# Gated linear attention and a multiplicative feed-forward on one core: smaller weight units, an earlier x, and the output weight converted in part 1

## The chip, the cores and the metric

One NeuronCore of one Trainium2 chip runs the whole program in one launch. The metric is device time in microseconds (us); lower is better. Engines are called PE (TensorE, matmuls; PEld is its weight load), DVE (VectorE), ACT (ScalarE), POOL (GpSimd) and SP (SyncE, which here only issues transfers).

## The reference

Shapes: batch 4, 8 heads, 768 steps, head dimension 48; then 3072 tokens of width 384 and a hidden width of 1024. The weights come as float64, the rest as float32.

```python
for t in range(S):                                   # per batch and head
    state = alpha[t][:, None] * state + outer(k[t], v[t])
    y[t]  = q[t] @ state
x = y.transpose(0, 2, 1, 3).reshape(3072, 384)       # heads side by side
h = ((x @ w1) * (x @ w2)) @ w3
out = h @ w_out
```

## The kernel before

The work falls into three stages.

**Part 1, attention by chunks.** The steps are cut into 24 chunks of 128 (`N = 24`, six for each batch). A chunk `n` goes through helpers that the loop `for n in range(N)` calls for different chunks at once:

- `load_a` and `load` fetch alpha, k, q and v, 192 KB each, in rows of 192 bytes, several chunks ahead.
- `logs` (ACT, L227) takes the logarithm of alpha; `decays` (PE L235, ACT L238 and L239) sums it along the chunk with a triangular matrix and exponentiates it both ways; `decayed` (DVE L247) multiplies k and q with that into `qk`.
- `transposed` (PE L266, ACT L267) turns `qk` into `qkT`.
- `scores` (PE L305, DVE L308) multiplies k with q and masks the result into `ms`.
- `outer` and `advance` (PE L277, DVE L285 and L287, POOL) carry the state to the next chunk.
- `attend` (PE L324 and L327, ACT L331) gives the chunk's output `x`; PE L324 is the product with the state and is left out in the first chunk of a batch.
- `store_x` writes `x` to a DRAM buffer `xd`, one for every three chunks (a group `g` of 384 tokens), from SP's queue, one chunk late.

**Weights.** The float64 weights are read as pairs of 32-bit words and put together again as float32 by `to_fp32` (DVE L180, L183, L186, L187, L189; ACT L179, L184). A unit is 128 rows by `CW = 512` columns of one matrix. For w1 and w2, `load_gates` then splits the result into three parts (ACT L196, DVE L198 and L199), so that three float32r products give the precision of float32. A unit is a generator: `convert(steps)` advances up to three begun units by so many steps, a gate unit taking four after its load and the others three. The six units of the first 512 columns (three blocks of rows for each matrix) are needed before the first gate tile.

**Gates.** `load_x(g)` reads a group back from `xd` as `xT`, `split_x` cuts it into three parts (ACT L352, DVE L353 and L354), and `gate(g, f)` computes 128 of the 1024 hidden columns: two halves (one for each of w1 and w2), each with six matmuls (PE L363), an evacuation (ACT L365), three matmuls (PE L367) and a second evacuation (DVE L368), then the product (DVE L379) that `store_ab` writes to DRAM. In part 1 the list `fill` holds gate tiles, and `run(1)`, called twice in a chunk, does half a tile each time. `begin` says after which chunk a group is split: groups 0 to 4 at chunks 6, 10, 14, 18 and 22.

**Part 2.** The remaining gate tiles are done one after another. Beside them the units of the output weight (`load_out`, eight) and of w3 (`load_w3`, sixteen) are converted, at 2.7 steps a tile. As soon as 128 rows of w3 are there, `fold` transposes them (PE L406, ACT L408) and multiplies them with `wo` (PE L412, split by ACT L415 and DVE L416 and L417), so that w3 and w_out become one matrix `w3o`. When all eight folds are done, `load_ab` begins to read the products back.

**Last part.** For each of 24 token blocks: `split_ab` (ACT L430, DVE L431 and L432) and `project` (PE L363 and L367 with `w3o`, DVE L368), and the store of the output.

Each engine works through its instructions in order. The framework's scheduler decides how the helpers' instructions are interleaved on an engine, so the order is close to the program's but not equal to it. Transfers from SP go through one queue, in order.

Of the kernel before, what the change touches and what calls it, by code (L numbers as in the profile page):

```python
# [20 lines left out]
P = 4096.0  # L21
# [27 lines left out]
def kernel(  # L49
# [36 lines left out]
    xp = pool("xp", 1)  # L86
    tr = [pool("tr0", 1)]
    gw = pool("gw", 2)
    abp = pool("abp", 3)
    dram = pool("dram", 1, space=DRAM)  # L90
    ps = pool("ps", 8, space=PSUM)
    conversion = ExitStack()
    rawp = pool("rawp", 3, stack=conversion, side="right")
    cvt = pool("cvt", 3, stack=conversion, side="right")
    part1 = ExitStack()
    p1 = pool("p1", 1, stack=part1, side="right", reuse_waits="tile")
    inp = pool("inp", 3, stack=part1, side="right", reuse_waits="tile")
# [24 lines left out]
            st["a", n] = inp.tile([C, H, D], FP32, tag="ac", name="ac")  # L122
            nc.sync.dma_start(out=st["a", n], in_=rows(alpha, n))

    def load(n):
        if n >= N:
            return
        st["kq", n] = inp.tile([C, 2, H, D], FP32, tag="kq", name="kq")
        st["v", n] = vs[n % len(vs)]
        nc.sync.dma_start(out=st["kq", n][:, 0], in_=rows(k, n))  # L130
        nc.sync.dma_start(out=st["kq", n][:, 1], in_=rows(q, n))
        nc.sync.dma_start(out=st["v", n][:, :, 0:D], in_=rows(v, n))

    nc.scalar.preload_act_table_set(LN_EXP_SET)
    load_a(0)
    load(0)
    load_a(1)
    load(1)
    load_a(2)


    ident = const.tile([C, C], FP32, name="ident")
    rebias = const.tile([C, 1], FP32, name="rebias")

    w12 = [const.tile([C, 3, KM, DF], FP32R, name=f"w{i + 1}") for i in range(2)]

    utri = p1.tile([C, C], FP32, name="utri")
    after = p1.tile([C, C], FP32, name="after")
# [15 lines left out]
    for x in Ts + decs:  # L164
        nc.gpsimd.memset(x, 0.0)

    def to_fp32(dst, src):

        n = src.shape[1]
        raw = rawp.tile([C, n], I64, tag="raw", name="raw")  # L170
        nc.sync.dma_start(out=raw, in_=src)
        yield
        words = raw.bitcast(U32).rearrange("p (n w) -> p n w", w=2)
        low, high = words[:, :, 0], words[:, :, 1]

        mant = cvt.tile([C, n], FP32, tag="mant", name="mant")
        top = mant.bitcast(U32)
        rest = cvt.tile([C, n], FP32, tag="rest", name="rest", bufs=2)
        nc.scalar.activation(rest, low, AF.Copy, scale=2.0 ** -52)  # L179
        nc.vector.tensor_scalar(top, high, 0x000FFFFF, 0x00100000, op0=ALU.bitwise_and, op1=ALU.bitwise_or)  # L180

        power = cvt.tile([C, n], U32, tag="power", name="power", bufs=2)
        nc.vector.tensor_scalar(power, high, 20, 0x7FF, op0=ALU.logical_shift_right, op1=ALU.bitwise_and)  # L183
        nc.scalar.activation(power, power, AF.Relu, scale=2.0 ** 23, bias=rebias)  # L184
        yield
        nc.vector.scalar_tensor_tensor(mant, top, 2.0 ** -20, rest, op0=ALU.mult, op1=ALU.add)  # L186
        nc.vector.scalar_tensor_tensor(power, high, 0x80000000, power, op0=ALU.bitwise_and, op1=ALU.bitwise_or)  # L187
        to = mant if dst is None else dst()
        nc.vector.tensor_mul(to, mant, power.bitcast(FP32))  # L189
        yield  # L190
        return to

    def load_gates(i, src, kk, c0, n):
        w = yield from to_fp32(None, src[ds(kk * C, C), ds(c0, n)])
        h, l, m = (w12[i][:, x, kk, ds(c0, n)] for x in range(3))
        nc.scalar.activation(h, w, AF.Copy, scale=(1.0 - 2.0 ** -13) / P)  # L196
        yield
        nc.vector.scalar_tensor_tensor(l, h.bitcast(FP32), -P, w, op0=ALU.mult, op1=ALU.add)  # L198
        nc.vector.scalar_tensor_tensor(m, h.bitcast(FP32), P + 1.0, w, op0=ALU.mult, op1=ALU.subtract)  # L199

    weights, begun = deque(), deque()

    def convert(steps):

        for _ in range(steps):
            while weights and len(begun) < 3:
                begun.append(weights.popleft())
                next(begun[-1])
            if not begun:
                return  # L210
            x = begun.popleft()
            try:
                next(x)
                begun.insert(min(1, len(begun)), x)
            except StopIteration:
                pass
# [14 lines left out]
    def decays(n):  # L231
# [2 lines left out]
        lc = bank()[:, 0:DM]  # L234
        nc.tensor.matmul(lc, utri if n % 2 else after, st.pop(("la", n)), start=True, stop=True)  # L235

        e = st["e", n] = work.tile([C, 2, DM], FP32, tag="e", name="e", bufs=3)
        nc.scalar.activation(e[:, 0], lc, AF.Exp, scale=-1.0)  # L238
        nc.scalar.activation(e[:, 1], lc, AF.Exp)  # L239
        if n in ends:  # L240
# [70 lines left out]
    def attend(n):  # L311
# [17 lines left out]
        st["x", n] = work.tile([C, HP, 2, C], FP32, tag="x", name="x")  # L329
        for i in range(2):  # L330
            nc.scalar.copy(st["x", n][:, :, i], y[i])  # L331

    def store_x(n):
        if n < 0:
            return
        x = st.pop(("x", n)).rearrange("p j i t -> p (j i) t")

        g, c = divmod(n, G)
        to = xd[g].rearrange("(b h d) t -> b d h t", b=2, d=D)
        for half in range(2):  # L340
            nc.sync.dma_start(out=to[half, :, :, ds(c * C, C)], in_=x[ds(DP * half, D)])


    def load_x(g):
# [25 lines left out]
    def gate(g, f):  # L370
        r = []
        x = [[st["x3", g][:, part, kk, :] for kk in range(KM)] for part in range(3)]
        for w, scale in zip(w12, (1.0, P * P)):
            r.append(gw.tile([C, TG], FP32, tag="r", name="r"))
            exact(r[-1], [[w[:, part, kk, ds(f * C, C)] for kk in range(KM)] for part in range(3)], x, scale)
            if len(r) == 1:
                yield
        ab = abp.tile([C, TG], FP32, tag="ab", name="ab")
        nc.vector.tensor_mul(ab, *r)  # L379
        store_ab()  # L380
        st["ab"] = g, f, ab
# [70 lines left out]
                fill.popleft()  # L452

    FH = CW // C
    for c0 in range(0, DF, CW):
        for kk in range(KM):
            for m, src in enumerate((moe_w1, moe_w2)):
                weights.append(load_gates(m, src, kk, c0, CW))

    logs(0)  # L460
    decays(0)
    decayed(0)
    logs(1)
    decays(1)
    transposed(0)
    load(2)
    load_a(3)
    decayed(1)
    logs(2)
    convert(1)  # L470
    decays(2)
    load(3)
    load_a(4)
    convert(2)
    logs(3)
    convert(1)

    begin = {6 + 4 * g: (g, range(FH if g < 4 else KF)) for g in range(5)}
    for n in range(N):
        load_a(n + 5)  # L480
        load(n + AHEAD)
        scores(n)
        convert(1)
        run(1)
        store_x(n - 1)
        advance(n)
        outer(n)
        transposed(n + 1)
        decayed(n + 2)
        logs(n + 4)  # L490
        convert(2)
        run(1)
        decays(n + 3)
        load_ends(n + 2)
        convert(1)
        attend(n)
        if n + 2 in begin:
            load_x(begin[n + 2][0])
        if n in begin:
            g, tiles = begin[n]  # L500
            split_x(g, 0)
            fill.extend(gate(g, f) for f in tiles)
    store_x(N - 1)
    part1.close()


# [2 lines left out]
    w3o = w3op.tile([C, 3, KF, DM], FP32R, name="w3o")  # L509
    folding = ExitStack()  # L510
    foldp = pool("foldp", 1, stack=folding, side="right", reuse_waits="tile")
    wo = foldp.tile([C, KF, DM], FP32, name="wo")
    folds, folded = deque(), 0
    for j in range(KF):
        weights.append(load_out(j))
    for i in range(KF):
        for c0 in range(0, DF, CW):
            weights.append(load_w3(i, c0))
# [9 lines left out]
    for i, x in enumerate(todo):  # L528
# [3 lines left out]
                load_x(order[0][2])  # L532
        for _ in x:
            pass
        owed += 2.7 if folds or folded else 1.2
        convert(int(owed))
        owed -= int(owed)
        if folded < KF:
# [2 lines left out]
                folded += 1  # L541
        elif lastp is None:
            folding.close()
            conversion.close()
            lastp = pool("lastp", 1, reuse_waits="tile")
            for n in range(4):
                load_ab(n)
# [37 lines left out]
```

## Time and profile before

| | |
|---|---|
| time, median of 3 | 510.59 us (509.92 to 510.64) |
| span of the profiled execution | 508.0 us |
| mean granted clock of PE | 0.982 |
| PE waiting for ACT `la` L227 | 12.3 us in 5 waits, the longest 4.4 |
| PE waiting for ACT `x` L352 | 4.9 us in 1 wait |
| bytes moved | 79.07 MB, 112664 of 167005 packets under 512 bytes |

The page lists busy time by engine and cuts the span into 40 slices, each digit the busy share in tenths. A table of stages gives the same for chosen stretches. In the order of time a row reads: start, length, engine, line, operation, output and inputs, count, and in brackets the idle time before it and what ended it. Instructions are pipelined: a group's mean duration is longer than the distance from one start to the next.

### The profile page before, as it was taken

Reading aid. Unit: us, or ns where it says so; the run is one execution under the profiler, and the core shown is the slowest. Engines: PE = TensorE matmul, PEld = TensorE weight load, DVE = VectorE, ACT = ScalarE, POOL = GpSimd, SP = SyncE. Lnnn points to the kernel's source line nnn. Section 1 sums busy time; section 2 is a strip of 40 time slices with the busy share of each in tenths; the row PEclk is TensorE's granted clock in tenths of the full one; section 3 lists DMA queues with packets and bytes.
Section 4 is the critical chain, followed back from the end, with each engine's and each line's share of the span. In section 5 each row is a group of like instructions: output and inputs, shape, how many; then the busy total and the mean of one; then the engine's idle time right before and its main releaser. Section 6 shows DMA issues by size and latency. Waiting matters only on the chain.

```text
span 508.0 us, 9443 instructions
## 1 busy us (share of the span) xinstructions
PE 483.0 (95%) x3568; PEld 429.2 (84%) x3568; DVE 367.2 (72%) x606; ACT 245.0 (48%) x465; POOL 16.6 (3%) x41
## 2 busy tenths in 40 slices
PE   4979769999999999999999999999999999999996
PEld 2657558878888888999999988888888999999996
DVE  2599988985655674899999866976433967777761
ACT  3577746664545564446556544444322533333330
POOL 1031000100000100000000000000000000000000
PEclk9979959999999999999999999999999999999999
DMA  9999898988998751566554633320002855565511
GB/s 159 245 180 204 194 241 195 236 158 198 177 209 171 205 160 42 161 177 187 181 186 162 192 115 114 115 88 33 31 32 91 250 155 179 173 184 175 173 53 46
DMA packets 167005, 79.07 MB, mean 156 GB/s; under 512 B 112664, under 2 KB 162352, under 8 KB 166960
## 3 DMA queue, kind: packets, MB, share of 16 engines
q1 hardware_dynamic: 157440, 78.40, 59.8%
q10 hardware_dynamic: 9520, 0.07, 1.1%
q8 instruction: 28, 0.46, 0.4%
q14 instruction: 17, 0.14, 0.1%
HBM read 56.40 MB, written 22.06 MB: 154 GB/s over the span
## 4 chain that ended last, share of the span: by engine, by line
PE 78%; DVE 0%; issue 0%; DVEq 0%
PE bank L363 38%; PE bank L367 19%; PE bank L412 8%; PE bank L327 3%; PE bank L305 3%; PE bank L266 2%; PE bank L406 1%; PE bank L324 1%; PE bank L235 1%; PE bank L277 1%; DVE o L368 0%; DVEq L368 0%
## 5 line engine op out<-in xcount | busy, mean ns | idle before, releaser
L363 PE MATMUL bank<-x,w 128*128 128x384 f32 x768 | 163.1, 347 | 5.6 <-ACT x L352 4.9
L363 PEld LDWEIGHTS bank<-x,w 128*128 128x128 f32 x768 | 134.4, 190 | 10.8 <-ACT x L352 5.1
L365 ACT ACTIVATE t<-bank 128x384 f32<-128x384 f32 x152 | 74.0, 490 | 125.0 <-PE bank L363 113.3
L368 DVE SCALAR_TENSOR_TENSOR r<-bank,t 128x384 f32<-128x384 f32 x128 | 68.8, 552 | 49.9 <-ACT t L365 40.0
L367 PE MATMUL bank<-x,w 128*128 128x384 f32 x384 | 88.2, 337 | 1.7 <-DVE x L354 1.6
L367 PEld LDWEIGHTS bank<-x,w 128*128 128x128 f32 x384 | 68.6, 189 | 3.0 <-DVE x L354 2.7
L363 PE MATMUL bank<-w3o,ab 128*128 128x384 f32 x384 | 70.4, 334 | 0.0
L363 PEld LDWEIGHTS bank<-w3o,ab 128*128 128x128 f32 x384 | 66.9, 188 | 0.0
L412 PE MATMUL bank<-wo,w3T 128*128 128x384 f32 x128 | 42.6, 486 | 0.0
L179 ACT ACTIVATE rest<-raw 128x512 f32<-128x512 uint32 (+1 forms) x36 | 23.4, 649 | 32.1 <-DMA raw<-in_moe_w_dram 27.0
L367 PE MATMUL bank<-w3o,ab 128*128 128x384 f32 x192 | 37.1, 334 | 0.0
L412 PEld LDWEIGHTS bank<-wo,w3T 128*128 128x128 f32 x128 | 24.2, 189 | 14.9
L431 DVE TENSOR_TENSOR ab<-abl,ab 128x1024 fp32r<-128x1024 f32 x24 | 29.4, 1224 | 10.1 <-ACT ab L430 10.1
L379 DVE TENSOR_TENSOR ab<-r 128x384 f32<-128x384 f32 x64 | 35.4, 554 | 1.1
L308 DVE TENSOR_TENSOR ms<-bank,keep 128x512 int32<-128x512 int32 x48 | 31.1, 683 | 6.9 <-PE bank L305 6.7
L267 ACT COPY qkT<-bank 128x512 f32<-128x512 f32 x48 | 26.2, 587 | 18.9 <-PE bank L266 18.8
L430 ACT ACTIVATE ab<-abl 128x1024 fp32r<-128x1024 f32 x24 | 25.5, 1062 | 19.1 <-PE bank L367 18.8
L367 PEld LDWEIGHTS bank<-w3o,ab 128*128 128x128 f32 x192 | 33.6, 188 | 0.0
L247 DVE TENSOR_TENSOR qk<-kq,e 128x768 f32<-128x768 f32 x24 | 22.9, 953 | 14.6 <-ACT e L239 14.6
L184 ACT ACTIVATE power<-power,rebias 128x512 uint32<-128x512 uint32 (+1 forms) x36 | 25.0, 698 | 13.7 <-DVE power L183 13.5
L368 DVE SCALAR_TENSOR_TENSOR o<-bank,t 128x384 f32<-128x384 f32 x24 | 13.4, 557 | 24.4 <-issue 15.2
L266 PE MATMUL bank<-ident,qk 128*128 128x128 f32 x192 | 28.9, 298 | 0.9 <-DVE ms L308 0.8
(59 smaller groups left out, 523.3 us busy)
## 6 DMA issues: line engine op xcount, KB each, us to landing
raw<-in_moe_w_dram SPq DMA_DIRECT2D x28, 512.0 KB
abd<-ab SPq DMA_DIRECT2D x64, 192.0 KB
abl<-abd SPq DMA_DIRECT2D x24, 512.0 KB
xT<-xd SPq DMA_DIRECT2D x12, 576.0 KB
ac<-in_alpha_dram SPq DMA_DIRECT2D x24, 192.0 KB
kq<-in_k_dram SPq DMA_DIRECT2D x24, 192.0 KB
kq<-in_q_dram SPq DMA_DIRECT2D x24, 192.0 KB
v<-in_v_dram SPq DMA_DIRECT2D x24, 192.0 KB
```

The lines of the kernel that those rows point to most:

```text
L184: nc.scalar.activation(power, power, AF.Relu, scale=2.0 ** 23, bias=rebias)
L266: nc.tensor.transpose(tp[:, ds(j * C, C)], qk[:, i, 2 * j:2 * j + 2, :], ident)
L267: nc.scalar.copy(qkT[:, i], tp.rearrange("p (j c) -> p j c", j=NP))
L308: nc.vector.tensor_tensor(ms[:, i].bitcast(I32), sc[i].bitcast(I32), keep_bc, op=ALU.bitwise_and)
L363: nc.tensor.matmul(p1, w[part][i], x[part][i], start=(part == i == 0), stop=(part == 1 and i == n - 1))
L365: nc.scalar.activation(t, p1, AF.Copy, scale=(1.0 + 1.0 / P) * scale)
L367: nc.tensor.matmul(p2, w[2][i], x[2][i], start=(i == 0), stop=(i == n - 1))
L368: nc.vector.scalar_tensor_tensor(to, p2, -scale, t, op0=ALU.mult, op1=ALU.add)
L379: nc.vector.tensor_mul(ab, *r)
L412: nc.tensor.matmul(po, w3T[:, j, :], wo[:, j, :], start=(j == 0), stop=(j == KF - 1))
L430: nc.scalar.activation(t[:, 0], ab, AF.Copy, scale=1.0 - 2.0 ** -13)
L431: nc.vector.tensor_sub(t[:, 1], ab, t[:, 0].bitcast(FP32))
```

## The change

Weights of the gates are converted in units of 256 columns of both matrices at once, so that a unit still holds 512 elements per partition; `w12` becomes one tile with an axis for the matrix. Groups are split two chunks earlier (4, 8, 12, 16, 20), ahead of `attend` in the loop, and read back after the chunk before. `x` is stored at the end of `attend`, from ACT's queue. The first loads are put in the order in which they are used: v is loaded apart from k and q, and one chunk later. The units of the output weight follow those of the gates in part 1, in a pool of their own; `convert` is called with other counts, and part 2 advances 1.2 steps a tile throughout. `abp` has two buffers in place of three, and `e` likewise. Its purpose is to open the gates earlier and to even out the conversions over the parts.

```diff
-    abp = pool("abp", 3)
+    abp = pool("abp", 2)
...
+    fold1 = ExitStack()
+    wo = pool("wop", 1, stack=fold1, side="right").tile([C, KF, DM], FP32, name="wo")
...
     nc.scalar.preload_act_table_set(LN_EXP_SET)
     load_a(0)
-    load(0)
+    load_kq(0)
     load_a(1)
-    load(1)
+    load_v(0)
+    load_kq(1)
     load_a(2)
...
-    w12 = [const.tile([C, 3, KM, DF], FP32R, name=f"w{i + 1}") for i in range(2)]
+    w12 = const.tile([C, 3, 2, KM, DF], FP32R, name="w12")
...
-        nc.sync.dma_start(out=raw, in_=src)
+        for i, src in enumerate(srcs):
+            nc.sync.dma_start(out=raw[:, ds(i * m, m)], in_=src)
...
-        e = st["e", n] = work.tile([C, 2, DM], FP32, tag="e", name="e", bufs=3)
+        e = st["e", n] = work.tile([C, 2, DM], FP32, tag="e", name="e")
...
-            nc.sync.dma_start(out=to[half, :, :, ds(c * C, C)], in_=x[ds(DP * half, D)])
+            nc.scalar.dma_start(out=to[half, :, :, ds(c * C, C)], in_=x[ds(DP * half, D)])
...
-    for c0 in range(0, DF, CW):
+    for c0 in range(0, DF, CW // 2):
         for kk in range(KM):
-            for m, src in enumerate((moe_w1, moe_w2)):
-                weights.append(load_gates(m, src, kk, c0, CW))
+            weights.append(load_gates(kk, c0, CW // 2))
+    for j in range(KF):
+        weights.append(load_out(j))
...
-    begin = {6 + 4 * g: (g, range(FH if g < 4 else KF)) for g in range(5)}
+    begin = {4 + 4 * g: (g, range(FH if g < 4 else KF)) for g in range(5)}
     for n in range(N):
+        load_v(n + AHEAD - 1)
         load_a(n + 5)
-        load(n + AHEAD)
+        load_kq(n + AHEAD)
         scores(n)
-        convert(1)
+        if n == 0:
+            logs(2)
+            decays(2)
+            logs(3)
+        convert(1, 2 if n == 0 else 3)
         run(1)
-        store_x(n - 1)
         advance(n)
         outer(n)
         transposed(n + 1)
         decayed(n + 2)
         logs(n + 4)
-        convert(2)
+        convert(2 if 2 < n < 7 else 1)
         run(1)
         decays(n + 3)
         load_ends(n + 2)
-        convert(1)
-        attend(n)
-        if n + 2 in begin:
-            load_x(begin[n + 2][0])
+        convert(1 if n < 7 else n % 2)
         if n in begin:
             g, tiles = begin[n]
             split_x(g, 0)
             fill.extend(gate(g, f) for f in tiles)
-    store_x(N - 1)
+        attend(n)
+        if n + 1 in begin:
+            load_x(begin[n + 1][0])
...
-    wo = foldp.tile([C, KF, DM], FP32, name="wo")
...
-    for j in range(KF):
-        weights.append(load_out(j))
...
-        owed += 2.7 if folds or folded else 1.2
+        owed += 1.2
```

## The prediction

> **What bounds the kernel now.** I read the page first (busy shares and slices), then a table of stages, then TensorE's waits, then the order of time where it still waits.
>
> ```profile
> PE 483.0 (95%) x3568; PEld 429.2 (84%) x3568; DVE 367.2 (72%) x606; ACT 245.0 (48%) x465; POOL 16.6 (3%) x41
> ...
> PE   4979769999999999999999999999999999999996
> ...
> DVE  2599988985655674899999866976433967777761
> ...
> DMA  9999898988998751566554633320002855565511
> ```
>
> TensorE (PE) is full from the ninth slice on (a slice is 12.7 us). The time to win lies in the first 110 us. The stages, with busy us of PE, weight load, DVE, ACT, POOL, then clock and DMA share:
>
> ```profile
> 0.00:12.00 12.00, 4.55 (x10) 2.32 (x11) 3.26 (x8) 3.96 (x7) 2.38 (x17) 1.00 1.11 158
> 12.00:22.00 10.00, 8.90 (x56) 6.03 (x56) 4.12 (x8) 5.06 (x10) 0.00 (x0) 1.00 1.23 264
> 22.00:37.00 15.00, 11.43 (x128) 8.91 (x124) 14.26 (x27) 10.78 (x23) 4.83 (x3) 0.77 0.97 168
> 37.00:61.00 24.00, 22.24 (x301) 16.33 (x300) 23.35 (x42) 18.24 (x40) 2.26 (x3) 1.00 0.95 218
> 61.00:77.00 16.00, 9.93 (x58) 8.19 (x59) 13.36 (x21) 8.00 (x16) 0.95 (x3) 0.68 0.98 211
> 77.00:105.00 28.00, 28.00 (x320) 23.17 (x320) 26.35 (x49) 19.34 (x43) 1.97 (x3) 1.00 0.91 206
> ...
> 115.00:203.00 88.00, 88.00 (x952) 74.64 (x953) 53.26 (x89) 47.10 (x102) 4.20 (x12) 1.00 0.74 167
> 203.00:290.00 87.00, 86.95 (x532) 85.95 (x529) 82.88 (x155) 46.59 (x87) 0.00 (x0) 1.00 0.57 179
> ```
>
> From 22 to 61 us VectorE (DVE) is busy 37.61 of 39 us and the transfers 95% or more: both are at their limit and PE follows. Later PE is full at full clock, and DVE's load (82.88 of 87 at 203 to 290) is hidden. The longest wait of PE after the start and its effect, in order of time:
>
> ```profile
> 61.58 0.38 SPq L346 DMA_DIRECT2D xT<-xd  x1
> ...
> 65.72 1.16 ACT L352 ACTIVATE x<-xT 128x1152 fp32r<-128x1152 f32 x1 [0.45 <-DMA xT<-xd]
> ...
> 66.91 1.36 DVE L353 TENSOR_TENSOR x<-xT,x 128x1152 fp32r<-128x1152 f32 x1 [0.19 <-ACT x L352]
> ...
> 66.94 2.72 PE L363 MATMUL bank<-x,w 128*128 128x384 f32 x6 [4.87 <-ACT x L352]
> ...
> 70.80 1.33 PE L367 MATMUL bank<-x,w 128*128 128x384 f32 x3 [1.14 <-DVE x L354]
> ```
>
> The first gate matmul waits 4.87 us for x, read back at 61.58. It then runs at half clock (2.72 us for six; 1.31 when warm) until about 77.
>
> PE's lost time is the span less its work at full speed. A chunk with two half gate tiles takes 8.36 us in the steady stretch (scores at 129.83 to scores at 138.19), without the state update 7.6, without the inter-chunk product 7.8. Adding what stands before each point: 29.6 us are lost by 66.94, 5 more in the slow stretch to 77, and 2 around 107, where a split of x reaches DVE late. After that nothing: PE does 353.1 us of work from the scores of chunk 17 (154.91) to the end of the span.
>
> **What the Trainium skill says.** "TensorE: Matmul & The Clock Gate", Part 1, says that an idle window of about 3.4 us halves PE's clock. The trace agrees: 0.68 after 4.87 us idle. "DMA: Bandwidth & Descriptors", Issuing engines are not separate DMA queues, says that transfers from SP and ACT run on the same 16 engines and interleave. So storing x from ACT frees SP's queue and saves no bandwidth; the trace of before, which stores from SP, does not show it. "Perfetto Trace Analysis", Identifying the Most-Contended Engine, warns that matmul busy time flatters PE; so I count work by start-to-start times.
>
> **The change part by part.** For DVE I use start-to-start times of queued instructions in the order of time, some 0.08 us under the durations: 0.60 for 128x512 forms (0.33 for the two bit operations), 0.87 qk, 1.27 each half of an x split, 0.47 for 128x384, 0.27 for a state update. A unit of gate weights then costs 3.67 us, one of output weight 1.93, one of w3 2.47.
>
> *Units of 256 columns.* The same 12 units of 512 elements per partition: no work is saved. But the first gate tiles need three units, not six. In the instruction order of before, DVE does this before its first split: 9 qk (7.8), 16 masks (9.6), 6 states (1.6), some 8 units (28.2), start-up 1.8, sum 49.0 us. It happened at 66.9, so DVE had lost 18. In the changed order: 8 qk (6.9), 12 masks (7.2), 5 states (1.3), nearly 5 units (17.2), start-up 1.8, sum 34.4. With the lag of 16 us that DVE holds between 37 and 61 us, it reaches the split at 50.4.
>
> *The transfers up to x.* From the packet records a 192-byte packet takes 17.6 ns, so a load of 192 KB takes 1024 x 17.6 / 16 = 1.13 us; a raw unit takes 1.7. Ahead of the first x load SP's queue of before holds 60.0 us of transfers, x itself included, and ACT met x at 65.7. The changed queue holds 46.6, plus 3 for four chunks stored from ACT: 10.5 us less, so x at about 55. The price for the smaller 2 KB rows of raw is not in the trace; I take the same bytes at the same rate (the lower bound) and leave up to 2 us in the range. The 16.3 ns per packet of the first 12 us would give 51. I take the split of x on ACT at 53.4 and the first gate matmul at 54.5.
>
> *What PE has done by then.* Before, seven chunks and the scores of the eighth; after, five and the scores of the sixth: 8.8 us of work less. The gates start 66.9 - 54.5 = 12.4 earlier, so PE's lost time falls by 3.6. PE's last work ahead is scores(5), which wait behind the masks of chunk 4 (DVE work 27.6 + 16 = 44), near 48; 6 us of idling follow, so the half-clock loss of 5 stays.
>
> *From there to the scores of chunk 17.* PE: 8 x 8.36 + 2 x 7.6 + 2 x 7.8 - 1.1 = 96.5, plus 5 for the clock. DVE from split to masks(17), counted in the order: 11 qk 9.6, 24 masks 14.4, states 2.7, four splits 10.2, 24 gate evacuations 11.2 and 12 products 5.6, rest of gate units 26.9, all eight wo units 15.4, begun w3 4.7: 100.7 us. Both are full; I add 1.5 for waiting on one another. Scores(17) come at 54.5 + 96.5 + 5 + 1.5 = 157.5. Two more gate tiles are done by then (four halves of 1.56 = 6.2 that part 2 no longer does), so the point to compare with is 154.9 + 6.2 = 161.1: 3.6 gained, the 2 us of the late split among them.
>
> *Output weight in part 1.* 15.4 us of DVE leave 203 to 290, where PE was full anyway, so they gain nothing there. They go into the DVE sum above, beside PE.
>
> *Conversion at 1.2 steps a tile.* The last fold now stands one gate tile before the end of the gates (3.1 us), not four. Before, the fold ended at 391.3, the first ab was split on ACT at 394.8 and PE came at 404.1, with room. Now the load is issued 1.5 us into the fold of 5.2 us. ACT splits it behind the last tile's evacuation, 1.2 us after PE's last gate matmul. I add 1.3.
>
> *The rest.* The x stores cost ACT two issues of about 0.45 a chunk; ACT is busy 19.34 of 28, so they are hidden. An ACT instruction held by a store's issue would delay the next qkT copies and through them transposes and masks; that is in the 1.5. Two buffers for ab and e hold: ab is reused two tiles (6.2 us) later, e after its qk product, which is already earlier in the order. The first loads bring alpha of chunk 1 one load earlier (1.1 us), swallowed by the transfer queue.
>
> Sum: -3.6 + 1.3 = -2.3 us, so 510.6 - 2.3 = 508.3.
>
> **The rivals.**
> A (the forecast, 0.36): 506.5 to 509.8.
> B (0.26), slower: DVE becomes the bound of all of part 1. For: 100.7 us of DVE beside 101.5 of PE, and at 77 to 105 it fell 2 us behind while 94% busy. At 94% over that stretch, scores(17) come at 55.5 + 107 = 162.5: 1.4 later than to compare, with the tail +2.7, so 513.3. Against: at 37 to 61 it ran at 97%.
> C (0.20), faster: transfers do not hold x back; DVE opens the gates at 51.4, 3 us earlier: 505. Against: DMA share 0.95 or more throughout.
> D (0.08), slower: the tail stall reaches the whole chain of about 6 us from fold to first ab, less 3.1, and over 3.4 us idle halves the clock: some 5 us on A, 513.5. Against: the load's waits end before the fold does.
> E (0.10), same: x at 56 and 2.5 of waits: 510.6.
>
> **How the numbers follow.** Faster: A less 0.02 near its upper end, and C: 0.54. Same: E and that 0.02: 0.12. Slower: B and D: 0.34. The range runs from C with a milder clock loss (501.5) to B with 2 us of later x (514.5).
>
> **What would show it.** Right: the first gate matmul at 53 to 56, after an idle of about 6 us and at half clock; DVE over 95% busy from 60 to 155; scores(17) near 157.5; PE idle 1 to 2 us before the first projection. Wrong: gates at 58 or later (transfers), scores(17) beyond 161 with waits on DVE (B), or over 3 us idle before the projection (D).

## The result and the profile after

The changed kernel takes 515.95 us (median of 4 runs, 514.33 to 518.47), the kernel before 510.25 beside it: ratio 1.0117, interval 1.007 to 1.0164. It is slower by about 6 us, where 508.3 was forecast. Medians, ratios and ranges are of fast runs; three runs (two of a kernel below and one of the kernel before, at 793.57 us) took over 1.5% more than the fastest of their kernel and are left out. The profiled execution took 518.47, so sizes read from its trace can be some 2.5 us above those of the median.

The stages of the changed kernel, in the columns used for before (stretch, length, busy us and instructions of PE, weight loads, DVE, ACT and POOL, PE's clock, DMA share, GB/s):

```profile
37.00:61.00 24.00, 18.38 (x150) 13.91 (x150) 19.52 (x33) 13.09 (x26) 1.71 (x3) 0.74 1.03 231
61.00:77.00 16.00, 16.00 (x169) 13.55 (x168) 15.68 (x30) 12.33 (x27) 0.75 (x3) 1.00 1.15 223
77.00:105.00 28.00, 26.67 (x284) 21.90 (x283) 24.60 (x44) 17.88 (x38) 1.93 (x4) 1.00 1.06 219
...
115.00:203.00 88.00, 82.66 (x822) 68.40 (x819) 68.07 (x125) 52.41 (x112) 4.22 (x11) 0.94 0.80 189
203.00:290.00 87.00, 87.00 (x595) 80.06 (x594) 67.80 (x122) 41.97 (x78) 0.51 (x1) 1.00 0.42 134
```

The slow stretch of PE has moved forward, from 61 to 77 us to 37 to 61, as the change wanted. DVE has 15 us less at 203 to 290 and 15 more at 115 to 203. But where PE of before was busy 88.00 of 88 us at clock 1.00, it is now busy 82.66 at 0.94. The first gates, in order of time:

```profile
47.86 2.46 SPq L350 DMA_DIRECT2D xT<-xd  x1
54.08 1.16 ACT L356 ACTIVATE x<-xT 128x1152 fp32r<-128x1152 f32 x1 [2.63 <-DMA xT<-xd]
55.27 1.36 DVE L357 TENSOR_TENSOR x<-xT,x 128x1152 fp32r<-128x1152 f32 x1 [0.57 <-ACT x L356]
55.29 0.79 PE L367 MATMUL bank<-x,w 128*128 128x384 f32 x3 [3.37 <-ACT x L356]
56.69 1.33 PE L367 MATMUL bank<-x,w 128*128 128x384 f32 x3 [0.60 <-DVE x L357]
58.04 1.30 PE L371 MATMUL bank<-x,w 128*128 128x384 f32 x3
...
61.47 0.69 PE L371 MATMUL bank<-x,w 128*128 128x384 f32 x3
```

x lands near 54 and the first gate matmul is at 55.29, against 66.94 before. So the loss comes later. The scores of chunk 17 are at 164.7, not at 157.5; those of chunk 23 at 216.2, where the forecast's sums give 205.2 (202.6 of before, plus 6.2 for two more gate tiles, less 3.6). Two chunks hold most of these 11 us, both with a split of x in them: from scores(13) to scores(14) it took 14.1 us (before 8.3), from scores(17) to scores(18) 11.6 (before 7.6). The first of them, with ScalarE's queue and the engines in order of time:

```profile
117.94 0.63 ACT L339 COPY x<-bank 128x256 f32<-128x256 f32 x2
118.60 0.87 ACTq L345 DMA_DIRECT2D xd<-x  x2
120.91 0.86 ACTq L263 DMA_DIRECT2D dec<-ends  x2
121.81 0.49 ACT L369 ACTIVATE t<-bank 128x384 f32<-128x384 f32 x1 [3.24 <-DMA xd<-x]
...
125.44 1.17 ACT L356 ACTIVATE x<-xT 128x1152 fp32r<-128x1152 f32 x1
...
126.65 0.79 PE L367 MATMUL bank<-x,w 128*128 128x384 f32 x3 [0.96 <-ACT x L356]
...
127.67 1.35 DVE L357 TENSOR_TENSOR x<-xT,x 128x1152 fp32r<-128x1152 f32 x1
...
129.07 1.33 PE L367 MATMUL bank<-x,w 128*128 128x384 f32 x3 [1.63 <-DVE x L357]
...
134.25 1.65 PE L367 MATMUL bank<-x,w 128*128 128x384 f32 x6
```

Between the copy that ends at 118.57 and the evacuation at 121.81 (L369), which waits for no transfer itself, ScalarE stands 3.24 us. The issues of the x store (0.87 us) and of the decay's loads (L263, 0.86 us) take 1.73 us of it; the other 1.44, from 119.47 to 120.91, is a wait ahead of L263. What L263 waits for is in the program's instruction list, where transfers of SP and ScalarE take turns on one set of completion counters, and an issue also waits for its counter's last user:

```
Activation L263 DMACopy dec1<-ends14
   wait DMAHW3 >= 304  -> SP L178 DMACopy raw<-in_moe_w_out_dram
   wait DMAHW4 >= 304  -> Activation L249 DMACopy ends14<-e
```

By the packet records the row of ends14 was written by 118.81, and the packets of the raw output weight ran until 121.25: two loads, one behind the other, of which L263 waits for one. The issue came at 120.91. So, by the list and the packets, ScalarE waited for a load of the output weight that its own transfer has nothing to do with. The releaser that the profile infers, a store of x, ended at 122.3 and can't be it. The split of x on ScalarE then comes 3.6 us later, behind conversion steps. VectorE reaches its half at 127.67, PE gets it at 129.07, and the three matmuls take 1.33 us: half clock.

The second of these chunks has another cause. No issue holds ScalarE ahead of its split; VectorE, which waited 1.53 us for raw weights at 160.37, reaches its half of the split late, and PE then waits for VectorE:

```profile
160.37 0.43 DVE L187 TENSOR_SCALAR mant<-raw 128x512 uint32<-128x512 uint32 x1 [1.53 <-DMA raw<-in_moe_w_dram]
...
164.71 1.15 ACT L356 ACTIVATE x<-xT 128x1152 fp32r<-128x1152 f32 x1
...
166.65 1.37 DVE L357 TENSOR_TENSOR x<-xT,x 128x1152 fp32r<-128x1152 f32 x1
...
168.07 0.80 PE L367 MATMUL bank<-x,w 128*128 128x384 f32 x3 [1.37 <-DVE x L357]
```

How much of the loss is idling and how much slow matmuls shows against the best version below, which does the same matmuls. From scores(6) to scores(23), the changed kernel and then the best version:

```profile
64.40:216.20 151.80, 144.71 (x1484) 120.03 (x1482) 120.85 (x218) 90.13 (x192) 7.40 (x18) 0.97 0.85 194
```

```profile
66.50:207.50 141.00, 138.57 (x1485) 116.49 (x1482) 106.08 (x179) 82.21 (x177) 7.61 (x18) 1.00 0.86 182
```

Of 10.8 us more, 6.1 are matmuls that take longer (144.71 busy against 138.57) and 4.7 idling. What ScalarE waited for, in us in total, times and the longest (20 to 220 us):

```profile
ACT rest L186 <- DMA raw<-in_moe_w_dram: 11.2, 11, 2.7
ACT t L369 <- DMA xd<-x: 5.3, 2, 3.2
...
ACT t L369 <- DMA ac<-in_alpha_dram: 2.5, 2, 1.6
```

Two kinds of transfers hold it: raw weights that it converts itself (L186), and transfers that only an issue in its queue waits for. The view counts the time that the issuing itself takes in these rows too.

### The profile page after: what moved, and what is told of

The parts are those of the page before. It is cut to its first block, busy times and chain, and to the rows that moved or that the text cites. A ratio compares the mean times of both kernels' runs of the same rounds, so it can differ in the third digit from the quotient of the medians.

```text
span 516.7 us, 9463 instructions
## 1 busy us (share of the span) xinstructions
PE 487.6 (94%) x3568; PEld 431.9 (84%) x3568; DVE 369.5 (72%) x606; ACT 245.4 (47%) x465; POOL 12.4 (2%) x41
## 4 chain that ended last, share of the span: by engine, by line
PE 66%; ACT 0%; DVE 0%; issue 0%; DVEq 0%
PE bank L367 34%; PE bank L371 17%; PE bank L416 8%; PE bank L335 1%; PE bank L410 1%; PE bank L274 1%; PE bank L313 1%; PE bank L332 1%; PE bank L285 1%; PE bank L243 0%; ACT ab L434 0%; DVE o L372 0%; ACT t L369 0%; DVEq L372 0%
## 5 line engine op out<-in xcount | busy, mean ns | idle before, releaser
L369 ACT ACTIVATE t<-bank 128x384 f32<-128x384 f32 x152 | 74.0, 490 | 139.5 <-PE bank L367 116.3
L186 ACT ACTIVATE rest<-raw 128x512 f32<-128x512 uint32 (+1 forms) x36 | 23.3, 649 | 28.7 <-DMA raw<-in_moe_w_dram 24.8
L274 PE MATMUL bank<-ident,qk 128*128 128x128 f32 x192 | 31.5, 317 | 3.7 <-DVE qk L255 3.7
L313 PE MATMUL bank<-qkT 48*128 48x128 f32 x384 | 29.5, 296 | 4.5 <-ACT qkT L275 4.5
L313 PEld LDWEIGHTS bank<-qkT 48*128 48x128 f32 x384 | 24.8, 198 | 9.7 <-ACT qkT L275 6.1
L191 ACT ACTIVATE power<-power,rebias 128x512 uint32<-128x512 uint32 (+1 forms) x36 | 25.0, 697 | 14.7 <-DVE power L190 13.1
```

The costliest lines, as they stand in the source:

```text
L274: nc.tensor.transpose(tp[:, ds(j * C, C)], qk[:, i, 2 * j:2 * j + 2, :], ident)
L313: nc.tensor.matmul(sc[i][:, j, :], qkT[r, 0, j, :], qkT[r, 1, j, :], start=True, stop=True)
L369: nc.scalar.activation(t, p1, AF.Copy, scale=(1.0 + 1.0 / P) * scale)
```

## The experiments

Three theories were set against each other. V: the conversions taken into part 1 fill VectorE, and the splits and masks come late (the prediction's rival B). S: ScalarE is held at the issues of the x stores. R: the 2 KB rows and the late raw loads hold the engines. Ratios are to the kernel before, beside it on the same chip; a ratio of 0.001 is 0.51 us. "VectorE's work ahead of masks(17)" is counted in each kernel's own instruction order with the prediction's prices: 110.6 us before, 135.2 after. It matters since the scheduler moves conversions when something else changes.

Counted in the changed kernel's trace from scores(6) to scores(23), S is not so to the letter: ahead of the 34 issues of x stores ScalarE waits 0.04 us at most, and the 6.3 us that it waits at issues are all at those of the decay's rows and loads. But issuing alone occupies it for 16.6 us there, 11.7 of them for the x stores; on before, with the x stores on SP, it is 4.4 us from scores(8) to scores(23), without a wait.

**The output weight back in part 2.** On the changed kernel:

```diff
-    wo = pool("wop", 1, stack=fold1, side="right").tile(...)
-    for j in range(KF):          # ahead of part 1
-        weights.append(load_out(j))
+    wo = foldp.tile([C, KF, DM], FP32, name="wo")
+    for j in range(KF):          # behind part1.close()
+        weights.append(load_out(j))
-        owed += 1.2
+        owed += 2.7 if folds or folded else 1.2
```

> The changed kernel with the output weight converted in part 2 again, its tile in the folding pool and 2.7 steps a tile, all else as changed. In the instruction order VectorE now has 119.6 us of work ahead of masks(17), against 135.2 in the changed kernel. Theory V (conversions taken into part 1 fill VectorE, so splits of x and masks come late): scores(17) at 156 to 159 instead of 164.7, the split of group 3 no longer makes PE wait, total 506 to 511. Theory S (ScalarE is held at the issues of the x stores, whatever VectorE does): scores(17) still beyond 162, total 514 or more. Theory R (2 KB rows and late raw loads hold VectorE): the splits of groups 1 and 2 remain late, scores(17) about 162, total 513 to 515.

Measured 512.19 us, ratio 1.0027 (1.001 to 1.0043): 4.6 us of the 6 come back, and 1.4 us above before are left. The total is in none of the three forecasts. Scores(17) at 163.5 is not what V forecast, scores(23) at 211.0 is 5.2 earlier than in the changed kernel. From there to the end it takes 299.1 us, the changed kernel 300.5: 1.4 of the 4.6 us are the tail. VectorE now has room, and ScalarE still stands 3.18 us, 2.90 of them waiting:

```profile
109.48 0.24 ACTq L235 DMA_DIRECT2D ends<-ac  x1
109.76 0.49 ACT L367 ACTIVATE t<-bank 128x384 f32<-128x384 f32 x1 [3.18 <-DMA ac<-in_alpha_dram]
```

This time it is data: L235 stores a row of alpha, and its load, issued from SP at 103.85, is late among the others. The scheduler has put the store into ScalarE's queue ahead of work that needed nothing of it. So S has to be put wider: any issue in ScalarE's queue can hold it, for its own data or for its counter.

**The x stores from SP**, with the output weight in part 1, and in part 2:

```diff
-            nc.scalar.dma_start(out=to[half, ...
+            nc.sync.dma_start(out=to[half, ...
```

> The changed kernel with the x stores issued from SP at the same place, output weight still in part 1. The instruction order moves with it: VectorE has 119.8 us of work ahead of masks(17), not 135.2, as later conversions slide behind. Theory S: ScalarE's waits on transfers go, 5 to 8 us of delay of gates and masks go, total 508 to 511. Theory V: total 508 to 512 because of the order alone. So this run alone does not tell them apart; total above 514 would be against both.

> Both: output weight in part 2 and x stores from SP. VectorE's order is that of the run with the output weight alone undone (119.6 us ahead of masks(17)), so the difference of the two is the store's engine alone. Theory V: within 1.5 us of that run. Theory S: 4 us or more below it. Theory R: at most 1 us.

Measured 0.9988 (0.9971 to 1.0006; 510.33 us) and 0.9971 (0.9955 to 0.9986; 509.44 us). With the x stores on SP the changed kernel is 6.6 us faster, and the one with the output weight in part 2 2.9. But the order moved both times: VectorE's work ahead of masks(17) falls from 135.2 to 119.8 us in the first pair, and from 119.6 to 115.9 in the second, where the expectation had 119.6. So neither pair tells the engine from the order. x also comes later: scores(6) at 68.9 instead of 64.4. After that the run loses nothing: 92.7 us from scores(6) to scores(17), where the run with ScalarE's stores needs 99.1.

**The stores of group 0 alone from ScalarE, later ones from SP**, with the output weight in part 2 and in part 1:

```diff
-            nc.scalar.dma_start(out=to[half, ...
+            (nc.scalar if g == 0 else nc.sync).dma_start(out=to[half, ...
```

> Output weight in part 2; the x stores of group 0 (chunks 0 to 2) issued from ScalarE, all later ones from SP. VectorE has 115.9 us of work ahead of masks(17), the order of the run with all stores on SP. That run lost 4.5 us before scores(6) (68.9 against 64.4) because x came late, and then took 92.7 us to scores(17), against 99.1 with all stores on ScalarE. Theory S with the early x as the store's gain: scores(6) at 64 to 65, scores(17) at 157 to 158, total 504 to 507. If the stores of group 0 are themselves what holds ScalarE: scores(6) at 66 or later, total 508 to 510.

> The changed kernel, output weight in part 1, with the stores of group 0 alone on ScalarE and the later ones on SP. VectorE: 119.8 us of work ahead of masks(17), but all 8 output-weight units by masks(23). Against the run above, the difference is the output weight alone. Theory V: it costs 2 to 4 us by scores(23), total 507 to 510. If the output weight is harmless once ScalarE is free: within 1 us of the run above.

Measured 506.7 us, 0.9917 (0.989 to 0.9944), and 509.21 us, 0.9973 (0.9957 to 0.9989). The first beats both kernels. Its scores(6) came at 66.5, where the expectation had 66 or later go with a higher total, scores(17) at 160.0. The split of group 2, which cost PE most in the changed kernel, now takes 10.0 us from scores(13) to scores(14) instead of 14.1. ScalarE waits 1.19 us for x itself, and PE 0.60 for VectorE's half:

```profile
124.87 1.16 ACT L354 ACTIVATE x<-xT 128x1152 fp32r<-128x1152 f32 x1 [1.19 <-DMA xT<-xd]
126.07 1.36 DVE L355 TENSOR_TENSOR x<-xT,x 128x1152 fp32r<-128x1152 f32 x1 [0.50 <-ACT x L354]
...
127.48 0.80 PE L365 MATMUL bank<-x,w 128*128 128x384 f32 x3 [0.60 <-DVE x L355]
...
130.92 1.31 PE L365 MATMUL bank<-x,w 128*128 128x384 f32 x6
```

Six matmuls take 1.31 us right after: full clock. With the output weight in part 1 it is 2.9 us slower (0.9973 less 0.9917). Of these, 1.4 are the tail; up to scores(23) the profiled executions show no loss (207.2 us against 207.5). So a VectorE as full as in the changed kernel (121.4 us busy from scores(6) to scores(23)) need not cost PE time before the tail.

**The x stores from GpSimd**, output weight in part 2. Here the sum of VectorE's work ahead of masks(17) stays (119.6 us), though the order within it doesn't: by the two traces the split of group 2 stands four instructions sooner on VectorE and two sooner on ScalarE. So this pair comes nearest to a change of the issuing engine alone, but is not quite that.

```diff
-            nc.scalar.dma_start(out=to[half, ...
+            nc.gpsimd.dma_start(out=to[half, ...
```

> Output weight in part 2, all x stores issued from GpSimd's queue. VectorE's order is that of the run with the output weight alone undone up to masks(17) (119.6 us), so this pair differs in the issuing engine alone. Theory S: ScalarE waits on no transfer ahead of its evictions, scores(17) at 157 to 159, total 505 to 508. Theory V (the order makes the difference): total 510.5 to 513.5. An issue on GpSimd that is itself slow would show as x later than 55 us.

Measured 0.9949 (0.9932 to 0.9966; 507.98 us) against 1.0027: 4.0 us for moving the issues off ScalarE, with what moved in the order. The total is in the range that S named. Scores(17) came at 162.8, later than S forecast, but the profiled execution took 510.75 us, 2.8 above the median. In its trace the time that ScalarE waits at issues did not fall (9.4 us, 8.8 in the first run); the time that it spends issuing did, from 20.2 to 5.8. Which of issuing and order gives the 4.0 us isn't shown.

**Single parts put on the kernel before.** The output weight in part 1 (own memory, queued behind the gate weights, two buffers for ab and e); the x stores at once from ScalarE; two buffers alone; units of 256 columns alone:

```diff
+    wo = pool("wop", 1, stack=fold1, side="right").tile(...)   # first kernel
-            nc.sync.dma_start(out=to[half, ...                 # second, without store_x(n - 1)
+            nc.scalar.dma_start(out=to[half, ...
-    abp = pool("abp", 3)                                       # third, and e likewise
+    abp = pool("abp", 2)
-    for c0 in range(0, DF, CW):                                # fourth, with load_gates of the change
+    for c0 in range(0, DF, CW // 2):
```

> The kernel before with only the output weight taken into part 1 (own memory, queued behind the gate weights; two buffers for ab and e to make room). VectorE has 126.0 us of work ahead of masks(17), against 110.6. Theory V: VectorE of before idled 21 us between 77 and 155 us, 15.4 of which this fills; splits of groups 1 to 3 come late by 1 to 3 us each: 511 to 515. Theory S and theory R: no effect, 509.5 to 511.

> The kernel before with its x stores alone moved: at once in attend, from ScalarE. VectorE has 114.2 us of work ahead of masks(17), against 110.6. Theory S: x a little earlier, but ScalarE held by 1 to 3 us at a time on transfers, waits of the kind evicted-bank behind a DMA in its queue; total 513 to 517. Theory V: 509 to 511.5.

> The kernel before with two buffers for ab and for e instead of three, nothing else (the same edit stands in the run of before with the output weight in part 1). VectorE's order is the same but for one half microsecond. All theories: 510 to 511.5. Over 512 would mean that part of what was put down to the output weight there belongs to the buffers.

> The kernel before with the gate weights in units of 256 columns of both matrices, nothing else; VectorE's instruction order is unchanged, first gate after three units as well as six since begin stays at chunk 6. Theory R (2 KB rows cost transfer time while the queue is the limit): first gate matmul 1 to 2 us later than 66.9, total 511.5 to 513. Theories V and S: 510 to 511.5.

- The output weight: 517.62 us, 1.0133 (1.0105 to 1.0161), 6.8 us slower and beyond every expectation.
- The stores: 512.7 us, 1.005 (1.0034 to 1.0066). But its loss is ahead of chunk 8 (scores(8) at 82.4 against 79.4); from there to scores(23) it takes 123.5 us, before 123.1. The total lies between what V and S forecast.
- The buffers: 511.52 us, 1.0016 (1.0002 to 1.003). The first of these kernels has them too, so the output weight itself costs 6.0 of its 6.8 us.
- The units: 512.65 us, 1.0032 (1.002 to 1.0044). VectorE's order is that of before; the first gate matmul is at 69.5 instead of 66.94, but it is at 68.6 in the kernel with two buffers alone. From the packet records, 2048-byte packets take 117 ns each, 4096-byte ones 214 to 218: the 6 MB of gate weights cost an estimated 1.5 to 1.9 us more over the 16 engines. R is right on this, at about the size it named for the total.

**The sooner begin and the loads' order**, each undone on the best version:

```diff
-    begin = {4 + 4 * g: ...
+    begin = {6 + 4 * g: ...          # first kernel
...
-    load_a(1)                        # second: v beside k and q, alpha of chunk 1 behind
-    load_v(0)
...
+    load_v(0)
+    load_a(1)
```

> The best version so far (output weight in part 2, stores of group 0 alone on ScalarE) with the gates begun at chunk 6 again instead of chunk 4. The prediction's step: the sooner begin takes 3.6 us of lost TensorE time away, so this gives 509.5 to 511. If the gain comes from the loads or the units instead: 506 to 508.

> The best version so far with the loads of q, k, v and alpha in the order of the kernel before (v beside q and k, second alpha after the first chunk). VectorE's order is unchanged. The prediction's step (the order of the first loads is worth nothing once the transfer queue is full): within 0.7 us of 506.7. If the order of use is what brings x sooner: first gate matmul 1 to 2 us later and total 508 to 509.

Measured 1.002 (1.0005 to 1.0035; 511.39 us) and 0.9945 (0.9926 to 0.9965; 507.92 us), against 0.9917. The sooner begin is worth 5.3 us, more than forecast: begun at chunk 6, PE idles 11.5 us before its first gate matmul at 72.0. VectorE's order moved here too, by some 5 us of work ahead of masks(17). The order of the loads is worth about 1.4 us by the ratios, but the intervals overlap, and the first gate matmul comes no later with the old order (56.16 us, against 56.78); a gain isn't shown.

**Work without loads, loads without work.** The output weight in part 1 of the kernel before brings both. Eight conversions of one tile loaded once, or eight loads with no conversion, were added in part 1 (both with two buffers):

```diff
+    def again(j):                    # first: raw0 loaded once
+        yield from to_fp32(lambda: spare[:, j % 2, :], ..., raw0)
+    def again(j):                    # second
+        nc.sync.dma_start(out=raw, in_=moe_w_out[ds(j * C, C), :])
```

> The kernel before with two buffers for ab and e, and eight more conversion units of 384 columns in part 1 that all read one raw tile loaded once and write to a spare tile (work of VectorE and ScalarE without the loads; the real output weight stays in part 2, the result does not use the spare tile). VectorE has 126.0 us of work ahead of masks(17), as with the output weight in part 1. If the engines' work is what the output weight costs in part 1: 515.5 to 518.5, with TensorE waiting for splits of x around 140. If its transfers and raw buffers are: 511 to 512.5.

> The kernel before with two buffers for ab and e, and the eight loads of the output weight done in part 1 as well, at the same pace through the raw buffers, with no conversion (a load's data are dropped; the real output weight stays in part 2). VectorE has 110.1 us of work ahead of masks(17). If the engines' work is what the output weight costs: 510.5 to 512.5. If transfers are: 514 to 518.

Measured 0.9995 (0.9981 to 1.001; 510.69 us) and 1.0013 (0.9999 to 1.0028; 511.67 us). Neither costs anything against the two-buffer kernel (1.0016). The same stretch, 77 to 155 us, of before, of the kernel with the work, and of the one with the output weight:

```profile
77.00:155.00 78.00, 76.89 (x834) 63.98 (x832) 56.67 (x94) 44.99 (x99) 3.78 (x9) 1.00 0.93 196
```

```profile
77.00:155.00 78.00, 76.62 (x822) 63.53 (x822) 70.16 (x133) 51.78 (x116) 9.33 (x9) 1.00 0.96 201
```

```profile
77.00:155.00 78.00, 73.75 (x760) 61.05 (x758) 64.05 (x119) 47.57 (x105) 4.30 (x9) 0.96 0.93 207
```

VectorE busy 70.16 of 78 us with PE at 76.62, VectorE busy only 64.05 with PE at 73.75: on the kernel before, a full VectorE alone is not the cause, and V in its simple form falls there. In the last of these kernels the loss begins with ScalarE standing 3.95 us while the decay's loads wait to be issued. The wait is 2.33 us of this and the issuing 1.58. Their row, stored at 129.73, was written only at 132.94 by the packet records, beside a raw load of the output weight that ran until 131.54 and the packets of x read back:

```profile
133.60 1.58 ACTq L257 DMA_DIRECT2D dec<-ends  x2
135.22 0.55 ACT L181 ACTIVATE rest<-raw 128x384 f32<-128x384 uint32 x1 [3.95 <-issue]
...
140.61 1.16 ACT L354 ACTIVATE x<-xT 128x1152 fp32r<-128x1152 f32 x1
...
141.83 0.79 PE L365 MATMUL bank<-x,w 128*128 128x384 f32 x3 [1.44 <-ACT x L354]
143.69 0.84 PE L365 MATMUL bank<-x,w 128*128 128x384 f32 x3 [1.08 <-DVE x L355]
...
148.87 2.27 PE L365 MATMUL bank<-x,w 128*128 128x384 f32 x6
```

From 135.22 to 140.61 ScalarE works with one gap of 0.5 us, on ten instructions that are queued ahead of the split, four of them conversion steps; PE waits for the split and then runs at half clock (2.27 us for six). The kernel with the loads alone is held at the same issue for almost as long, but has no conversion step behind it:

```profile
133.71 1.14 ACTq L255 DMA_DIRECT2D dec<-ends  x2
134.95 0.49 ACT L365 ACTIVATE t<-bank 128x384 f32<-128x384 f32 x1 [3.70 <-PE bank L266]
...
136.90 1.16 ACT L352 ACTIVATE x<-xT 128x1152 fp32r<-128x1152 f32 x1
```

Its split comes at 136.90, behind three instructions, PE's six matmuls take 1.34 us at 140.16, full clock, and the four chunks from scores(14) to scores(17) take 25.1 us instead of 31.6. So a hold of 3.7 us costs PE nothing here without conversions queued behind it. That is one place in one execution of each kernel.

**All of ScalarE's issues moved to GpSimd**, on the changed kernel and on before with the output weight:

```diff
-            nc.scalar.dma_start(out=ends[n][2:3], in_=a[0:1])
+            nc.gpsimd.dma_start(out=ends[n][2:3], in_=a[0:1])   # likewise the other rows, decs; x in the first
```

> The changed kernel, output weight in part 1, with every transfer that ScalarE issues (x stores, the rows and values for the decay) issued from GpSimd instead. VectorE's order stays almost that of the changed kernel (134.2 us of work ahead of masks(17), against 135.2). If ScalarE held at its issues is the cause of the loss: scores(17) at 157 to 160, total 506.5 to 510. If VectorE's load in part 1 is, whatever ScalarE does: 513 to 517.

> The kernel before with the output weight in part 1, and the transfers for the decay, which ScalarE issues there, issued from GpSimd. In the run with ScalarE issuing them, ScalarE stood 3.95 us at one such issue, and TensorE lost 6.3 us at the next split of x. If that is the cause: scores(17) at 155 to 157, total 511 to 513.5. If work and loads together cost it by themselves: 515.5 to 518.5.

Measured 515.58 us, 1.0115 (1.0093 to 1.0137), and 512.75 us, 1.0053 (1.0032 to 1.0075). The second gives 4.1 of 6.8 us back, with runs from 508.92 to 516.53; its order of VectorE's work moved too, by some 2 us. The first gives nothing back: S alone falls too, and 515.58 lies in the range that V named for it. In the changed kernel V is therefore not excluded: of the 7.1 us that PE waits there from 61 to 220 us, VectorE ends 6.1 and ScalarE 1.0. The first also loads GpSimd, which carries the state: it is busy for 49.4 of 149 us with the issues and for 7.4 of 152 without, though no wait of PE ends with it. Its profiled execution (512.54 us, the fastest of six) shows what took the issues' place in ScalarE's waits (20 to 210 us):

```profile
ACT rest L186 <- DMA raw<-in_moe_w_dram: 12.4, 11, 2.8
...
ACT rest L186 <- DMA raw<-in_moe_w_out_dram: 7.2, 5, 3.4
```

**The best version with three buffers again, and then with the decay's transfers on GpSimd:**

```diff
-    abp = pool("abp", 2)
+    abp = pool("abp", 3)             # and e with bufs=3
```

> The best version so far with three buffers for ab and for e again (the output weight's memory in part 1 is free). VectorE's order is unchanged. If the third buffers were worth the 0.16% seen in the kernel before: 505.5 to 506.3; if that was chance: 506.3 to 507.2. At most 506.7 it beats both kernels.

> The best version so far with the transfers for the decay issued from GpSimd. VectorE's order is unchanged. ScalarE of the best version shows no wait on a transfer ahead of an eviction, so little is left: 505.5 to 507. If GpSimd's issues are slow enough to delay the decay: 507 to 510.

Measured 506.49 us, 0.9918 (0.99 to 0.9936), and 506.93 us, 0.9941 (0.9921 to 0.9961). Neither beats 0.9917; the buffers are worth nothing here, and taking the decay's issues off ScalarE gains nothing more.

**The runs side by side.** From scores(6) to scores(23) PE needs about 140.5 us if nothing stops it (the five kernels that lose least take 140.3 to 141.0). For one profiled execution of each kernel, what ScalarE stood in that stretch by the rows that the view puts down to transfers (raw loads and issues together, the issuing with them), VectorE's busy time, and the time lost:

| kernel | ScalarE waits, us | VectorE busy, us | lost, us |
|---|---|---|---|
| changed | 16.2 | 120.9 | 11.3 |
| changed, all issues on GpSimd | 15.8 | 121.5 | 8.2 |
| changed, x from SP | 16.9 | 121.6 | 5.8 |
| changed, x of group 0 on ScalarE | 7.9 | 121.4 | 1.6 |
| output weight in part 2 | 15.0 | 106.0 | 6.0 |
| same, x from GpSimd | 14.7 | 105.8 | 4.7 |
| same, x from SP | 4.8 | 105.8 | 0.1 |
| same, x of group 0 on ScalarE | 2.8 | 106.1 | 0.5 |

Where ScalarE waits under 8 us the loss is small even with a full VectorE; where it waits 15 us or more, it is 5 to 6 us with VectorE at 106 and 6 to 11 at 121. This is a weak pattern over single executions (16.9 us lost 5.8, and 15.0 lost 6.0), not an experiment on one cause.

## Why the prediction was wrong

**The step that failed.** "I add 1.5 for waiting on one another", in the sum from the first gates to scores(17), with whatever the x stores' issues hold left inside that 1.5, and the output weight's 15.4 us of VectorE taken to fit beside PE. From the first gate matmul at 55.29 to scores(17) at 164.73 it took 109.4 us in the profiled execution, where the sum has 103.0. With its other terms as they were, the 1.5 measured 7.9 us; scores(23) came 11.0 late against the forecast's sums. The rest of that sum holds in total: in the runs that lose least the same stretch takes 102.6 to 103.4 us. The loss reaches PE at the splits of x, since x has one buffer and the gate matmuls of a group wait for ACT's part of the split and then for VectorE's; and PE's clock falls with the idling.

The sum took the engines' work as what must fit. Taking the output weight out of part 1 gives 4.6 us (1.4 of them in the tail), and the x stores off ScalarE then another 4.0. On the kernel before with two buffers, the work alone and the loads alone cost nothing, and the real conversion, which has both, costs 6.0. There the traces show two things that multiply: an in-order queue held by a transfer, and conversions queued behind the hold, which use up the room in which it would be made good. For the changed kernel this is argued from the first of its two late chunks and not shown by a run that alters one thing alone.

"TensorE: Matmul & The Clock Gate", Part 1, of the Trainium skill has the idle window; the trace agrees with 1.33 us for three matmuls after the 3.37 us wait at 55.29, where three take 0.69 at full clock (at 61.47). But it also has 1.33 us at 129.07, after waits of only 0.96 and 1.63 us with three matmuls between them. There no wait is as long as that window, and the measurement decides: shorter waits with matmuls between them went with half clock too.

**An argument behind it that is in doubt.** The x stores' two issues of 0.45 us were priced rightly (0.87 us for a pair) and called hidden, since ScalarE is busy only 19.34 of 28 us. From scores(6) to scores(23) ScalarE waits ahead of none of these issues in the trace; but their 11.7 us there stand in the same queue as the decay's issues, which do wait, for their data or for another queue's load on their counter. In the place above the two together hold ScalarE for 3.24 us. That the x stores are not free there is measured (4.0 us with the output weight in part 2, with the order moved a little); how they cost it isn't shown.

**The rivals.** B ended on the right side with 513.3, and its picture came: VectorE is busy 93.64 us from 61 to 165 (90%), scores(17) come beyond 161, and PE's waits end with VectorE. As a cause it is half right: on the kernel before, the work without loads filled VectorE as far, 70.16 of 78 us, and cost nothing. C did not come, since the gates opened at 55.29 and not at 51.4, and D did not, since the tail took 1.4 us and not the whole chain.

**What held.** The first gate matmul (54.5 forecast, 55.29 measured), and half clock after a wait. The wait was 3.37 us, where about 6 were forecast, and full clock was back by 60.32, where six matmuls take 1.31 us again; so the 5 us for the clock were not seen at that size there. The gain of the sooner begin, in sign: 5.3 us where 3.6 was forecast, though the best version's begin at chunk 6 is itself later than before's (72.0 against 66.94). The tail: 1.3 forecast, 1.4 measured (300.5 less 299.1). The buffers of ab and e: nothing in the best version, 0.8 us on before (0.1 to 1.5).

**What was mis-sized.** The 2 KB rows were taken at the rate of 4 KB rows: they cost 1.6 us of the total when put on before alone, within the 2 us left for them in the range.

**What stays open.** How much of the raw loads' lateness in the changed kernel is SP's queue and how much the rate of the transfers, and why moving all of ScalarE's issues helps so little there, while moving the x stores alone gives 4.0 us with the output weight in part 2, and moving the decay's alone gives 4.1 on before with the output weight in part 1. A run of the changed kernel with VectorE's and ScalarE's orders held fixed, and only the issuing engine changed, was not made; it would tell issuing from order.

## What to carry to other kernels

Engine totals that fit side by side are not enough: ask which in-order queue can be held by a transfer (its own issue, or data it converts), and whether there is room behind it to make that good. Moving work into a stage takes that room away: at one place of the kernel before, a hold of 3.7 us cost nothing without conversions behind it, and with them it ended in a half-clock stretch. Compare the instruction orders before reading a pair of runs: here they moved when only the engine of a store was changed. Issue only those transfers from a computing engine whose early start is needed: storing group 0 from ScalarE and the rest from SP, with the output weight in part 2, gives 506.7 us, ratio 0.9917 to the kernel before; the changed kernel has 1.0117.

## What the runs showed of the hardware

- A 2048-byte packet takes 117 ns and a 4096-byte one 214 to 218: half the bytes cost 54 to 55% of the time.
- One row of 1536 bytes took 3.2 us from issue to written (129.73 to 132.94), beside a raw load and a read-back of x, and 1.6 us in the changed kernel (117.23 to 118.81). In the first case the issue that reads the row back began at 133.60, and ScalarE stood 2.33 us ahead of it.
- Issuing occupies the issuing engine: 0.87 us for ScalarE's two x stores, 0.86 to 1.58 for the decay's two loads.
- Kernels scatter by different amounts: 508.92 to 516.53 us in 20 runs of the one with the output weight in part 1 and the decay's issues on GpSimd, 508.31 to 512.44 in 29 runs of the kernel before beside it. The cause isn't shown.
